# Attention scores in chunks of 256 queries, and one full-array product for values and softmax sums

## The chip, the cores and the metric

The kernel runs on one core of a Trainium2 chip, as one launch. The metric is the device time of that core in microseconds (us). A core has five engines with their own instruction queues, which here do the following: TensorE (PE in the profile, with PEld for its weight loads) multiplies matrices, VectorE (DVE) and ScalarE (ACT) work on the results, GpSimd (POOL) issues the loads that convert types, and SyncE (SP) issues the other transfers. TensorE writes its results to PSUM, which has eight banks; one bank holds 512 fp32 numbers in each of 128 partitions. Each engine takes its instructions strictly in the order in which the program gives them to it.

## The reference

Eight batches of attention with eight heads, 576 positions, 64 numbers per head, and a bias that depends only on the distance between query and key; then a feed-forward layer whose hidden part is the maximum of three products.

```python
scores = (q @ k.transpose(0, 1, 3, 2)) / sqrt(64)          # 8 x 8 x 576 x 576
scores = scores + bias_table[bucket(|i - j|)]              # one number per distance and head
attn = exp(scores - max) ; attn = attn / attn.sum(-1)
x = (attn @ v)  as  4608 tokens x 512
h = maximum(maximum(x @ w1, x @ w2), x @ w3)               # 4608 x 768
out = h @ w_out                                            # 4608 x 512, fp32
```

## The kernel before

The kernel computes scores transposed: keys lie in the partitions and queries along the row, so that the exponentials can be the moving operand of the product with the values. The bias becomes a factor: exp(score) is multiplied by exp(bias), and since the bias is constant beyond a distance of 128, only a band of three 128-wide blocks needs the multiplication (`band`, made at the start from the table by way of `w_sb`, a DRAM buffer `w_dr` and the skewed reload `hank`).

The work goes by 32 pairs of heads: 8 batches times 4 head pairs. The 576 positions of a pair are four key tiles of 128 (`KT`) and a tail of 64 keys; the two heads' tails share the 128 partitions of one "tail" tile. Queries are cut into two halves of `QC` = 288. For one pair the program does this:

- `transpose_q` and `transpose_k` (L325 to L343): ten 128x128 transposes on PE into the PSUM tiles `tq` and `tk`, and two DVE copies to `qT` and `kT`.
- `scores` (L345): the tail tile gives two full-array products of 288 columns (`et`); each of the four key tiles times two query halves gives two products of 288 columns, one per head. Each head contracts over 64 partitions, so the two lie in the upper and lower half of the array's rows ("64\*128" in the profile) and run at the same time. One ACT instruction makes the exponential of 2 x 288 numbers (L363), and DVE multiplies the part within the band (L368, L375).
- `attend` (L386), once per query half: the sum of the exponentials (`den`, with weights of ones) and the product with the values (`o`). Each has one full-array product for the tail, then eight of 64 output columns ("128\*64"), two heads side by side in the array's columns, that run in pairs. ACT makes 1/den as exp(-ln(den)) (L404, L406) and DVE multiplies (L408) into `xT`, the input of the feed-forward.

The feed-forward works on nine chunks of 512 tokens (`ffn_units`, L255): 18 groups of four 512-column products (L90 `ps`), of which every third is copied by ACT (L274) and the others are joined by DVE with a maximum (L277, L280), and four groups of six products for the output, copied by DVE or ACT (L303, L305) and stored by SP. A chunk is cut into 96 single products, which `fill` pours between the pieces of attention by a table of rates; chunk n is poured while batch n + 1 is in attention, and the last two chunks stand at the end. TensorE's instructions are kept in the order in which the program writes them; a scheduler orders the other engines' instructions at build time.

PSUM: `ps_s` has two tiles of two banks for the scores, `ps_a` one bank each for `o` and `den` (used by the transposes too), `ps_f` two banks for the feed-forward.

## Time and profile before

| | us |
|---|---|
| median of 3 runs (415.25 to 417.08) | 415.8 |
| profiled execution, whole | 415.32 |
| its span, first to last instruction | 413.5 |
| PE busy in the span | 379.2 |
| DVE busy | 241.4 |
| ACT busy | 250.7 |
| one batch in the middle (four pairs), period | 44.75 |
| end part: the last two feed-forward chunks | 43.34 |

The profile gives, for a group of instructions, the line, the engine, the operation, output and inputs by the program's names, the shape, the count, the busy time, the mean length of one in ns, and the idle time in front of them with what ended it. A timeline row is a start, a length, and how many instructions are merged in it. Matmuls are pipelined: one of 512 columns is shown 380 ns long although the next starts sooner, so the spacing of starts, not the length, is what a matmul costs in a stream. Most matmuls have the line of a helper, L90, and are told apart by their tiles.

### The profile page before, as it was taken

The page shows a single profiled execution, that of the slowest core. Times are in us where ns is not written, and L with a number is a line of the kernel's source. Part 1 is how long each engine was busy: PE and PEld are TensorE (multiplying, and loading weights), DVE is VectorE, ACT ScalarE, POOL GpSimd, SP SyncE. Part 2 cuts the span into 40 slices and gives each one's busy share as a digit, 9 for nine tenths or more (in the row PEclk, how much of TensorE's full clock was granted, in tenths as well). Part 3 has the DMA queues.
Part 4 walks back from the last instruction along what each step waited for, and adds up shares of the span by engine and source line. Part 5 has one row for each costly group of instructions (what it writes and reads, how often), then busy time and mean ns, then how long its engine had stood idle before and what let it go on. Part 6 is the DMA issues. An engine that isn't in the chain of part 4 may idle for free.

```text
span 413.5 us, 7525 instructions
## 1 busy us (share of the span) xinstructions
PE 379.2 (92%) x2912; PEld 177.9 (43%) x2912; DVE 241.4 (58%) x589; ACT 250.7 (61%) x476; POOL 113.4 (27%) x147
## 2 busy tenths in 40 slices
PE   1488799999999999999999999999999999999995
PEld 1144444444444444444444444444444444444442
DVE  7653556566666665565656666666556565554342
ACT  1565866766766666766676667667676667732221
POOL 8893570804053131604080405312000000000000
PEclk9999999999999999999999999999999999999999
DMA  9999990946469290919094647928001100020202
GB/s 138 191 132 209 168 120 2 90 52 106 30 42 74 103 58 3 113 52 109 0 94 49 106 29 46 70 104 58 0 2 51 52 2 1 27 76 2 102 0 103
DMA packets 121931, 28.61 MB, mean 69 GB/s; under 512 B 113952, under 2 KB 117288, under 8 KB 121896
## 3 DMA queue, kind: packets, MB, share of 16 engines
q0 software_dynamic: 110544, 16.72, 56.3%
q1 hardware_dynamic: 11352, 11.42, 8.3%
q8 instruction: 23, 0.38, 0.4%
q14 instruction: 12, 0.10, 0.1%
HBM read 35.39 MB, written 9.45 MB: 108 GB/s over the span
## 4 chain that ended last, share of the span: by engine, by line
PE 81%; ACT 10%; DMA 2%; issue 2%; DVE 2%; SPq 1%; DVEq 0%
PE ps L90 43%; PE den L90 13%; PE sc L90 11%; PE o L90 9%; ACT e L363 6%; ACT m L274 3%; PE tk L93 2%; PE tq L93 2%; DMA hank<-w_dr 2%; DMA w_dr<-w_sb 1%; SPq L154 1%; ACT rd L406 1%; ACT ld L404 1%; SPq L149 0%; DVE kT L342 0%
## 5 line engine op out<-in xcount | busy, mean ns | idle before, releaser
L363 ACT ACTIVATE e<-sc 128x576 bf16<-128x576 f32 x256 | 152.3, 648 | 100.7 <-PE sc L90 100.5
L90 PE MATMUL ps<-xT,w_bf 128*128 128x512 bf16 x648 | 163.2, 380 | 9.8 <-ACT m L274 9.8
L375 DVE TENSOR_TENSOR e<-e,band 128x576 bf16<-128x576 bf16 (+5 forms) x224 | 80.0, 358 | 90.6 <-ACT e L363 84.7
L90 PEld LDWEIGHTS <-w_bf 128*128 128x128 bf16 x648 | 55.4, 97 | 86.2 <-issue 38.4
L90 PE MATMUL sc<-qT,kT 64*128 64x288 bf16 (+1 forms) x576 | 71.0, 297 | 11.7 <-DVE kT L342 6.1
L90 PEld LDWEIGHTS <-kT 64*128 64x128 bf16 (+1 forms) x576 | 21.9, 95 | 73.3 <-issue 59.5
L90 PE MATMUL ps<-wo_bf,hT 128*128 128x512 bf16 x216 | 52.8, 380 | 0.0
L118 POOL DMA_DIRECT2D q_sb<-in_q_dram x32 | 28.1, 889 | 84.2 <-PE tk L93 76.5
L277 DVE TENSOR_TENSOR m<-ps,m 128x512 bf16<-128x512 f32 x54 | 37.1, 687 | 22.2 <-PE ps L90 16.0
L408 DVE TENSOR_TENSOR xT<-o,rd 128x288 bf16<-128x288 f32 x64 | 29.3, 458 | 35.0 <-ACT rd L406 31.9
L274 ACT ACTIVATE m<-ps 128x512 bf16<-128x512 f32 x54 | 32.5, 602 | 22.2 <-PE ps L90 22.2
L90 PE MATMUL den<-e,ones 128*64 128x288 bf16 x512 | 44.6, 297 | 0.0
L90 PE MATMUL o<-e,v_sb 128*64 128x288 bf16 x512 | 43.1, 291 | 0.0
L280 DVE TENSOR_TENSOR hT<-ps,m 128x512 bf16<-128x512 f32 x54 | 37.1, 688 | 3.5
L122 POOL DMA_DIRECT2D vtail<-in_v_dram x18 | 11.1, 626 | 82.7 <-PE o L90 77.2
L90 PEld LDWEIGHTS <-ones 128*64 128x64 bf16 x512 | 23.9, 110 | 18.4 <-issue 17.0
L404 ACT ACTIVATE ld<-den 128x288 f32<-128x288 f32 x64 | 26.3, 412 | 8.7 <-PE den L90 8.7
L90 PEld LDWEIGHTS <-v_sb 128*64 128x64 bf16 x512 | 29.5, 112 | 2.8
L406 ACT ACTIVATE rd<-ld 128x288 f32<-128x288 f32 x64 | 28.3, 443 | 2.0
L90 PEld LDWEIGHTS <-hT 128*128 128x128 bf16 x216 | 18.5, 97 | 24.3 <-issue 7.0
L118 POOL DMA_DIRECT2D v_sb<-in_v_dram x32 | 28.5, 926 | 0.4 <-issue 0.4
L363 ACT ACTIVATE et<-sc 128x576 bf16<-128x576 f32 x32 | 21.2, 663 | 11.9 <-PE sc L90 11.1
(48 smaller groups left out, 242.3 us busy)
## 6 DMA issues: line engine op xcount, KB each, us to landing
out_dram<-osb SPq DMA_DIRECT2D x36, 256.0 KB, 2.0
q_sb<-in_q_dram POOLq DMA_DIRECT2D x28, 128.0 KB, 4.1
k_sb<-in_k_dram POOLq DMA_DIRECT2D x28, 128.0 KB, 4.0
v_sb<-in_v_dram POOLq DMA_DIRECT2D x28, 128.0 KB, 3.8
w_bf<-in_moe_w_dram POOLq DMA_DIRECT2D x3, 768.0 KB, 11.4
k<-in_k_dram SPq DMA_DIRECT2D x8, 128.0 KB, 3.5
wo_bf<-in_moe_w_out_dram POOLq DMA_DIRECT2D x1, 768.0 KB, 17.4
hank<-w_dr SPq DMA_DIRECT2D x1, 576.0 KB
```

Source lines behind the costliest of these rows:

```text
L90: tc.keep_in_program_order(nc.tensor.matmul(*args, **kw))
L93: tc.keep_in_program_order(nc.tensor.transpose(*args))
L118: nc.gpsimd.dma_start(out=dst[:, t, h0:h1, :], in_=x[:, t, h0:h1, :])
L122: nc.gpsimd.dma_start(out=dst[b % 2][64 * par : 64 * par + 64, h0 // 2 : h1 // 2, 64 * par : 64 * par + 64], in_=src[b, h0 + par : h1 : 2, ...
L274: nc.scalar.activation(out=st["m"][:], in_=ps[:], func=ACTF.Copy)
L277: nc.vector.tensor_tensor(out=m1[:], in0=ps[:], in1=st["m"][:], op=ALU.max)
L280: nc.vector.tensor_tensor(out=hT[:, cf, :], in0=ps[:], in1=st["m"][:], op=ALU.max)
L363: nc.scalar.activation(out=e[:], in_=sc[:, :, 0:QC], func=ACTF.Exp, scale=inv_sqrt_d)
L375: nc.vector.tensor_tensor(out=e[:, :, lo - c * QC : hi - c * QC], in0=e[:, :, lo - c * QC : hi - c * QC], in1=band[hp][:, :, lo - P * t + ...
L404: nc.scalar.activation(out=ld[:], in_=den[:, 0:QC], func=ACTF.Ln)
L406: nc.scalar.activation(out=rd[:], in_=ld[:], func=ACTF.Exp, scale=-1.0)
L408: nc.vector.tensor_tensor(out=xT[hp][:, x0 : x0 + QC], in0=o[:, 0:QC], in1=rd[:], op=ALU.mult)
```

## The change

Scores are computed in two "visits" per pair, each over 256 queries (`QS`), with two key tiles and both heads in one PSUM tile of two banks, so that one exponential takes 2 x 2 x 256 numbers. The 64 queries left over (`left_queries`) and the tail keys (`left_keys`) get products of their own over the full array. All exponentials of a pair go into one tile `e4`, which leaves `attend` free to read query halves of 288 as before.

The values are stored as `vx`: for each head 64 columns of values and 64 columns of ones beside them, so one full-array product gives both the sum over the values and the sum of the exponentials, in the two halves of the partitions of one bank per head (`a0`, `a1`). The tail's product is a pair of row-tiled ones (`attend_open`) put directly behind a visit, which is row-tiled too. The logarithm is now two ACT instructions over 64 partitions (L418), the last multiplication two DVE instructions (L423).

The pair order changes: a pair's two `attend` calls run in the next pair, one behind each visit. The transposes of q and k go to one score tile (`tp`) behind the second visit. The feed-forward is cut into portions of whole groups, of which one goes behind each visit's `attend`; `left_keys` or `left_queries` stands before the last group of the portion. A portion in the middle of a chunk is: third product of a hidden block (`second`), first product of the next (`first`), then, behind the left-over scores, the middle one (`middle`). The end part takes the first two products from the two-bank score tiles. The startup has more set in program order, k is cast partly by ACT, and the constants of the second buffer set are written later.

```diff
-    ep = ctx.enter_context(tc.tile_pool(name="ep", bufs=16))
-    etp = ctx.enter_context(tc.tile_pool(name="etp", bufs=3))
+    ep = ctx.enter_context(tc.tile_pool(name="ep", bufs=3))
...
+    def constants(i):
+        inorder(nc.vector.memset(qtail[i][:], 0.0))
+        inorder(nc.vector.memset(ktail[i][:], 0.0))
+        inorder(nc.vector.memset(vt[i][0:64, :, D:], 1.0))
+        inorder(nc.vector.memset(vt[i][64:128, :, 0:D], 1.0))
+        inorder(nc.vector.memset(vx[i][:].rearrange("p t (h c) -> p (t h) c", c=P)[:, :, D:], 1.0))
...
+    load_hank(0, 2)
+    load_k32(4, H)
+    load_hank(2, H)
...
+        portions = [[f[0], m[0]]] + [[g[cf - 1], f[cf], m[cf]] for cf in range(1, FCH)]
+        portions += [[g[-1], o[0]], o[1:3]]
+        return portions, o[3:]
...
+    def fill(between=None):
+        groups = pending.pop(0) if pending else []
+        for group in groups[:-1]:
+            group()
+        if between:
+            between()
+        for group in groups[-1:]:
+            group()
...
+    def transposes(b, hp):
+        tp = ps_s.tile([P, 2, 2 * CH], BF16, tag="sc", name="tp")
...
+    def visit(qT, kT, e4, c):
+        for tt in range(0, KT, 2):
+            sc = ps_s.tile([P, 2, 2, QS], F32, tag="sc", name="sc")
+            for t in range(2):
+                for par in range(2):
+                    r = slice(64 * par, 64 * par + 64)
+                    mm(
+                        sc[:, par, t, :], lhsT=kT[r, P * (tt + t) : P * (tt + t) + P],
+                        rhs=qT[r, c * QS : c * QS + QS],
+                    )
+            exp(e4[:, tt : tt + 2, :, c * QS : c * QS + QS].rearrange("p t h q -> p h t q"), sc[:])
+
+    def left_keys(qT, kT, et):
+        sc = ps_s.tile([P, 2 * CH], F32, tag="sc", name="sct")
+        kd = kT[:, KT * P :]
+        mm(sc[:, 0:QM], lhsT=kd, rhs=qT[:, 0:QM])
+        mm(sc[:, QM:S], lhsT=kd, rhs=qT[:, QM : QM + 64], start=True, stop=False)
+        mm(sc[:, QM:S], lhsT=kd, rhs=qT[:, QM + 64 : QM + 128], start=False, stop=True)
+        exp(et[:], sc[:, 0:S])
+
+    def left_queries(qT, kT, e4):
+        sc = ps_s.tile([P, KT, 2, 64], F32, tag="sc", name="scq")
+        for t in range(KT):
+            mm(sc[:, t, :, :], lhsT=kT[:, P * t : P * t + P], rhs=qT[:, QM : QM + P])
+        exp(e4[:, :, :, QM:S], sc[:])
+
+    def attend_open(b, hp, c, et):
+        x = [ps_a.tile([P, CH], F32, tag=f"a{par}", name=f"a{par}") for par in range(2)]
+        for par in range(2):
+            r = slice(64 * par, 64 * par + 64)
+            mm(
+                x[par][:, 0:QC], lhsT=vt[b % 2][r, hp, :], rhs=et[r, c * QC : c * QC + QC],
+                start=True, stop=False, skip_group_check=True,
+            )
+        return x
+
+    def attend(b, hp, c, x, e4):
+        for par in range(2):
+            v0 = (2 * hp + par) * P - 64 * par
+            for t in range(KT):
+                mm(
+                    x[par][:, 0:QC], lhsT=vx[b % 2][:, t, v0 : v0 + P],
+                    rhs=e4[:, t, par, c * QC : c * QC + QC], start=False, stop=(t == KT - 1),
+                    skip_group_check=True,
+                )
+        for par in range(2):
+            r, d = slice(64 * par, 64 * par + 64), slice(64 - 64 * par, 128 - 64 * par)
+            nc.scalar.activation(out=ld[r, :], in_=x[par][d, 0:QC], func=ACTF.Ln)
+        nc.scalar.activation(out=rd[:], in_=ld[:], func=ACTF.Exp, scale=-1.0)
...
-    RATES = (6.0, 3.0, 6.5, 4.0, 4.5)
...
+        visit(qT, kT, e4, 0)
+        if before:
+            x = attend_open(*before[0], 0, before[2])
+            attend(*before[0], 0, x, before[1])
...
+        times_band(hp, e4, 0, 0, QS)
...
+        fill(lambda: left_keys(qT, kT, et))
...
+        visit(qT, kT, e4, 1)
+        if before:
+            x = attend_open(*before[0], 1, before[2])
+            attend(*before[0], 1, x, before[1])
+        times_band(hp, e4, 1, 0, 3 * P)
+        times_band(hp, e4, 2, P, 4 * P)
...
+        if ahead:
+            nxt = transposes(*ahead)
...
+        fill(lambda: left_queries(qT, kT, e4))
+        times_band(hp, e4, 3, 2 * P, S)
```

The order of the instructions moves with it, and two places matter. The first is TensorE from the end of a run of scores into the product with the values, for a pair in the middle. In these rows `kT` holds the transposed keys, `ones` and `onesd` are the weights that sum, `vtail`, `vt` and `vx` are values. Before:

```order
L90 MATMUL sc<-qT,kT 128x288
L90 LDWEIGHTS onesd
L90 MATMUL den<-et,onesd 128x288
L90 LDWEIGHTS vtail_97
L90 MATMUL o<-et,vtail_97 128x288
L90 LDWEIGHTS ones
L90 MATMUL den<-e,ones 64x288
```

And now, at the same place, with `a_2074` and `a_2075` for the banks of the two heads:

```order
L94 MATMUL sc<-qT,kT 128x256
L94 LDWEIGHTS vt_96
L94 MATMUL a_2074<-et,vt_96 128x288
L94 LDWEIGHTS vt_96
L94 MATMUL a_2075<-et,vt_96 128x288
L94 LDWEIGHTS vx_94
L94 MATMUL a_2074<-e_1867,vx_94 128x288
```

The array's form goes from row-tiled to full to column-tiled before, and from row-tiled to full now; the tail's products have joined the row-tiled run.

The second place is VectorE from the last band multiplications of a pair to the end of the next feed-forward group. `hT` is the DVE maximum that empties the PSUM bank of a block's third product, `m` the one that empties the middle product's. Before, in the second half of a pair:

```order
L408 TENSOR_TENSOR xT_240<-o,rd 128x288
L280 TENSOR_TENSOR hT<-ps,m_1806 128x512
L375 TENSOR_TENSOR e<-e,band_195 128x2x224
L375 TENSOR_TENSOR e<-e,band_195 128x576
L332 COPY qT<-tq 128x576
L368 TENSOR_TENSOR et<-et,bandt_200 128x192
L342 COPY kT<-tk 128x640
L277 TENSOR_TENSOR m_1910<-ps,m_1867 128x512
L280 TENSOR_TENSOR hT<-ps,m_1910 128x512
```

And now, for a pair with feed-forward in both halves:

```order
L289 TENSOR_TENSOR m<-ps_1493,m_1486 128x512
L355 TENSOR_TENSOR e_1441<-e_1441,band_194 128x2x384 x2
L348 COPY qT<-tp 128x640
L348 COPY kT<-tp 128x640
L423 TENSOR_TENSOR xT_201<-a_1513,rd 64x288
L423 TENSOR_TENSOR xT_201<-a_1514,rd 64x288
L294 TENSOR_TENSOR hT<-ps_1549,m 128x512
L355 TENSOR_TENSOR e_1441<-e_1441,band_194 128x2x320
L289 TENSOR_TENSOR m<-ps_1568,m_1560 128x512
```

In the second half of a pair, the two largest band multiplications, both copies of the transposes and both final multiplications now stand in front of `hT`.

More of the change, by code (lines that the diff above doesn't have):

```diff
@@ L61 @@
     QC = S // 2
+    QS = 2 * P
+    QM = 2 * QS
     KT = 4
@@ L169, in load_tiles @@
         k_sb = loads.tile([P, KT, H, D], BF16, tag="k_sb", name="k_sb")
-        v_sb = loads.tile([P, KT, H, D], BF16, tag="v_sb", name="v_sb")
-        return q_sb, k_sb, v_sb
+        return q_sb, k_sb
     batch = [None] * B
@@ L241 @@
+    ready = {n: (n * CH + CH - 1) // S for n in range(NCH)}
+    pairs = [(b, hp) for b in range(B) for hp in range(HP)]
+    cast_k32(0, 2, act_copy)
+    nxt = transposes(0, 0)
+    cast_k32(2, 4, dve_copy)
+    constants(1)
     batch[1] = load_tiles()
-    load_q(1, 0, H, batch[1])
-    load_k(1, 0, H, batch[1])
+    load_q(1, 0, H)
+    load_k(1, 0, H)
     w_bf = []
@@ L410 @@
-    ready = {n: (n * CH + CH - 1) // S for n in range(NCH)}
-    RATES = (6.0, 3.0, 6.5, 4.0, 4.5)
-    pairs = [(b, hp) for b in range(B) for hp in range(HP)]
-    late = []
-    made, factors = [], []
-    nxt = (transpose_q(0, 0), transpose_k(0, 0))
+    before = None
     for i, (b, hp) in enumerate(pairs):
@@ L456 @@
-    fill(8)
-    while late:
-        late.pop(0)()
+            load_q(b + 2, 0, H)
+            load_k(b + 2, 0, H)
+        fill(lambda: left_queries(qT, kT, e4))
+        times_band(hp, e4, 3, 2 * P, S)
+        before = ((b, hp), e4, et)
+    for c in range(2):
+        x = attend_open(*before[0], c, before[2])
+        attend(*before[0], c, x, before[1])
+        fill()
     for n in range(NCH):
         if ready[n] == B - 1:
-            pending.extend(ffn_units(n))
+            add_ffn(n, True)
```

391 lines of the change are left out of this document (157 added, 234 removed).

## The prediction, made before the changed kernel had run

> **What bounds the kernel now.** I read the page first, then the busy times by stage, TensorE's timeline in the middle, the groups by shape, and the end of the chain that ended last. Of the page, the span, the busy line and the granted clock by slices:
>
> ```profile
> span 413.5 us, 7525 instructions
> PE 379.2 (92%) x2912; PEld 177.9 (43%) x2912; DVE 241.4 (58%) x589; ACT 250.7 (61%) x476; POOL 113.4 (27%) x147
> ...
> PEclk9999999999999999999999999999999999999999
> ```
>
> By stage, with PE, PEld, DVE, ACT and POOL busy in that order, one batch cut at its period:
>
> ```profile
> 189.75:234.50 44.75, 43.35 (x354) 20.38 (x352) 27.60 (x64) 30.26 (x58) 13.71 (x18) 1.00 0.69 64
> ```
>
> A batch takes 44.75 us, a pair 11.19, and PE is busy 43.35 of it: PE bounds. What a matmul costs there is in the spacing of starts. TensorE's timeline in that batch:
>
> ```profile
> 231.61 0.42 PE L90 MATMUL sc<-qT,kT 64*128 64x288 bf16 x4
> 231.96 0.30 PE L90 MATMUL den<-et,onesd 128*128 128x288 bf16 x1
> 232.09 0.29 PE L90 MATMUL o<-et,vtail 128*128 128x288 bf16 x1
> 232.31 0.68 PE L90 MATMUL den<-e,ones 128*64 128x288 bf16 x8
> 232.82 0.66 PE L90 MATMUL o<-e,v_sb 128*64 128x288 bf16 x8
> 233.41 0.82 PE L90 MATMUL ps<-xT,w_bf 128*128 128x512 bf16 x3
> 234.17 0.42 PE L90 MATMUL sc<-qT,kT 64*128 64x288 bf16 x4
> 234.52 1.25 PE L90 MATMUL ps<-xT,w_bf 128*128 128x512 bf16 x5
> 236.24 0.59 PE L90 MATMUL ps<-xT,w_bf 128*128 128x512 bf16 x2 [0.47 <-ACT m L274]
> ...
> 241.00 0.39 PE L93 MATMUL tq<-ident,q_sb 128*128 128x128 bf16 x4
> ...
> 241.56 1.46 PE L90 MATMUL ps<-xT,w_bf 128*128 128x512 bf16 x6
> ```
>
> And the end part, from the chain that ended last:
>
> ```profile
> 366.07 43.34 PE ps L90 x192
> ```
>
> A full-array product of 288 columns takes 0.13 (232.09 - 231.96). Eight `den` take 0.51, so two side by side share one pass of 0.13. One of 512 columns takes 0.216: 43.34 / 192 = 0.226 with that part's waits, and 0.13 x 512 / 288 = 0.23 at most; I take off the waits. Where the array's form changes, about 0.09 is lost: `o` to `den` 0.22 instead of 0.13, `o` to `ps` 0.59 instead of 0.51, two passes of scores 0.35 instead of 0.26, three `ps` before scores 0.76 instead of 0.65. The ten transposes take 0.56. A wait on ACT delays PE by 236.24 - 234.52 - 5 x 0.216 = 0.64. In the list of waits (total, times, longest) it is
>
> ```profile
> PE ps L90 <- ACT m L274: 9.8, 21, 0.5
> ```
>
> 21 times for 28 pairs with feed-forward: three in four.
>
> One pair before: four runs of scores at 0.35 and 0.09 to enter, 1.76; two `attend` at 0.13 + 0.22 + 0.51 + 0.59, 2.90; tail scores 0.25; transposes 0.56; 24 products of feed-forward 5.18; the wait 0.48. Sum 11.13, against 11.19.
>
> **What the change does to PE.** Two visits of four passes, each 0.128 x 256 / 288 = 0.114, are 0.91. The openers, row-tiled, add a pass per visit, 0.26. Sixteen full-array products of 288 columns at 0.125 are 2.00, as many passes as `den` and `o` took beside the tail's. The form changes four times, 0.36, instead of twelve. Left keys (640 columns) 0.28, left queries (512) 0.22, transposes 0.56, feed-forward 5.18. Sum 9.77, where it was 10.65 without the wait.
>
> The Trainium skill, TensorEngine Tiling, section When to Use Tiling, speaks against part of this: weights of 64 columns should be tiled side by side. By that rule alone the value products would double, 1.0 more per pair. But the ones in the other half replace the `den` products, and the rows above count the same passes.
>
> **What is late next.** The other engines' rows, by shape:
>
> ```profile
> L363 ACT ACTIVATE e<-sc 128x576 bf16<-128x576 f32 x256 | 152.3, 648 | 100.7 <-PE sc L90 100.5
> L274 ACT ACTIVATE m<-ps 128x512 bf16<-128x512 f32 x54 | 32.5, 602 | 22.2 <-PE ps L90 22.2
> L375 DVE TENSOR_TENSOR e<-e,band 128x576 bf16<-128x576 bf16 x64 | 29.3, 458 | 5.9 <-ACT e L363 0.5
> L406 ACT ACTIVATE rd<-ld 128x288 f32<-128x288 f32 x64 | 28.3, 443 | 2.0
> L404 ACT ACTIVATE ld<-den 128x288 f32<-128x288 f32 x64 | 26.3, 412 | 8.7 <-PE den L90 8.7
> L342 DVE COPY kT<-tk 128x640 bf16<-128x640 bf16 x32 | 15.4, 483 | 0.0
> L375 DVE TENSOR_TENSOR e<-e,band 128x320 bf16<-128x320 bf16 x32 | 10.4, 325 | 22.1 <-ACT e L363 22.0
> ```
>
> How soon one follows another, from a timeline of all engines:
>
> ```profile
> 192.01 0.42 PE L90 MATMUL sc<-qT,kT 64*128 64x288 bf16 x4
> 192.35 1.19 ACT L363 ACTIVATE e<-sc 128x576 bf16<-128x576 f32 x2 [0.91 <-PE sc L90]
> ...
> 194.36 0.46 DVE L408 TENSOR_TENSOR xT<-o,rd 128x288 bf16<-128x288 f32 x1 [0.52 <-ACT rd L406]
> 194.73 0.68 DVE L280 TENSOR_TENSOR hT<-ps,m 128x512 bf16<-128x512 f32 x1
> ```
>
> ACT starts 0.34 after the pass that it reads starts; its second exponential starts 0.10 before the first ends (2 x 0.648 - 1.19); DVE overlaps by 0.09. The trace has no exponential of 1024 numbers: ACT grows by (648 - 412) / 288 = 0.82 ns each, so 648 + 448 x 0.82 = 1.02. Band multiplications grow by (458 - 325) / 256 = 0.52 ns, so 768 numbers take 0.56. Both go beyond the largest shape seen; a rival below prices that.
>
> I follow a pair with feed-forward in both halves, from its first visit. PE: visit 0.46, opener 0.13, change 0.09, eight products to 1.68; `second` and `first` to 3.41; left keys 3.69; `middle` 4.55; second visit from 4.65; `attend` to 6.33; transposes 6.89; `second` and `first` 8.62; left queries 8.84; `middle` would end at 9.70, the next pair begin at 9.80.
>
> In the first half nothing stops PE. ACT has both exponentials done at 2.4, the logarithms (two now, 0.31 net each) and `rd` at 3.5; DVE's two final multiplications free `a0` and `a1` at 4.3, wanted at 5.1. `middle` takes the bank of `second`, which DVE empties by 3.4, wanted at 3.69. Closest is the ring of two score tiles: the second half of the second visit, at 4.88, needs the tail's exponential out; ACT copies `first` till 4.2, then does the tail till 4.77. It fits by 0.1.
>
> In the second half DVE's order decides. Its band multiplication for key tile 2 waits for the second visit's second exponential, which starts at 4.65 + 0.11 + 0.34 + 0.92 = 6.02 and ends at 7.04. Then DVE does, each less 0.09: the band 0.47, `qT` 0.40, `kT` 0.40, two final multiplications 0.37 each, from 7.07 to 9.08, and only then `hT`, to 9.77. PE's `middle` needs the bank that `hT` empties and stands in PE's queue from 8.84; it starts at 9.82, and all behind it is 0.98 late: 10.78. In a batch's first pair an output copy has `hT`'s place, with the same 10.78. The last pair's second half has ten products and no `middle`: 9.80 - 2 x 0.216 = 9.37. A batch takes 3 x 10.78 + 9.37 = 41.7, against 44.75.
>
> **The two ends.** DVE's first bands that wait for the second `hank`, and TensorE's start, with one `den` run in the first stage and one later, and the first tail scores of the third and fifth pair:
>
> ```profile
> 17.19 0.36 DVE L237 COPY band<-hank 128x768 bf16<-128x768 bf16 x1 [0.55 <-DMA hank<-w_dr]
> ```
> ```profile
> 26.27 1.17 PE L90 MATMUL den<-e,ones 128*64 128x288 bf16 x8
> ...
> 29.49 0.64 PE L90 MATMUL sc<-qT,kT 128*128 128x288 bf16 x2 [0.50 <-ACT e L363]
> ...
> 35.32 0.68 PE L90 MATMUL den<-e,ones 128*64 128x288 bf16 x8
> ...
> 51.02 0.40 PE L90 MATMUL sc<-qT,kT 128*128 128x288 bf16 x2 [0.68 <-ACT e L363]
> ```
>
> The second `hank` now stands behind six k loads on SP's queue and comes some 3 to 4 late, with the other bands behind it on DVE; so I leave the third pair at 29, although the first scores start earlier. Then the old order pays back five owed `attend`; the new one runs 8.5 to 9 a pair without feed-forward: ACT's work is four exponentials at 0.92, 1.0 for tail and left queries, 1.2 for logarithms and 0.9 for `rd`, 6.8, and about 2 go by while DVE makes the last multiplications and the copy that starts the next pair. Batch 1 begins at 47 instead of 51.0 (43 if the late `hank` costs nothing, 51 if it costs twice that). Its first pair has eight products of feed-forward, 8.6: batch 1 takes 39.5, to 86.5; six batches of 41.7 reach 336.8. Then come two `attend` 2.6, 18 products left over 3.9, 192 products 41.5 and a wait of 1.0 for the last pair's bands and banks: 385.8. After the last product 413.5 - 409.4 = 4.1 remain: span 389.9. The profiled execution was 415.32, 1.8 over its span, and 0.5 under the median: **392 us**.
>
> **Rivals.** (1) The stall at `middle` is much smaller, because copies and multiplications on DVE are shorter than these rows: 20 pairs x 0.98 less, 372. Against it: the order is fixed, and the rows are steady. 0.12. (2) The score ring closes: the 0.1 of slack at the tail's exponential is gone, because ACT reaches it 0.6 later; PE waits 0.5 in each of 28 pairs, 14 more, 406. For it: ACT is the engine with least room in that half. 0.20. (3) The exponential with reordered output is slow, and ACT and the chain behind it become the bound: at 1.6 us instead of 1.02 the second exponential ends 1.16 later, three pairs take 11.94, the last 10.2 by ACT's sum (four exponentials 6.0, tail and left queries 1.0, four logarithms 1.2, two `rd` 0.9, a copy and a half 0.9, gaps 0.2): 46.0 a batch, 7 x 4.3 = 30 more and some 4 in batch 0: 426, slower than before. It decides from about 1.45 on. Against it: runs of 256 stay contiguous. 0.08. (4) The clock falls back. The eight `den` at 26.27 take 1.17, those at 35.32 0.68, so PE ran at about half speed at first although the page grants full clock; a later wait of 0.68 (51.02) did not bring that back. If waits of 1 a pair did, with 3.4 us at half speed in each pair, 1.7 x 28 = 48 more: 440. The Trainium skill, TensorE: Matmul & The Clock Gate, Part 1, section on PSUM-queue depth-cycling, says that frequent small idles between groups can make the clock oscillate; no run here shows it. 0.02. (5) Ring and stall together eat the gain, or the start loses it: within 0.5% of 415.8. 0.05.
>
> **How the numbers follow.** The forecast has 0.53, with 382 to 400 from the start's bounds and 0.3 either way per pair. Half a per cent is about what a measurement here can tell. Faster: 0.53 + 0.12 + 0.20 = 0.85; same 0.05; slower 0.10. The range takes in rivals 1 and 2: 370 to 408.
>
> **What would show it.** Right: 41.7 a batch; PE waiting about 1 us for DVE's `hT` once in three pairs of four; four form changes a pair; exponentials of 1.02. Wrong: PE waiting before scores on ACT (2); exponentials of 1.4 or more (3); matmuls at double spacing in the middle (4); batch 1 starting after 51.

## The result, and the profile after

| | before | after |
|---|---|---|
| median of the runs compared, us | 415.58 (7525 instructions) | 402.88 (6692 instructions) |
| ratio, 95% interval | | 0.9685 (0.9652 to 0.9717) |
| profiled execution: whole, span | 415.32, 413.5 | 401.81, 400.0 |
| batch 1 begins in the span | 51.02 | 53.27 |
| one batch in the middle | 44.75 | 42.12 |
| from the end of the last batch, by its period, to the end of the span | 49.23 | 51.53 |

The change makes the kernel 3.15% faster (2.8 to 3.5). The table says where: seven batches give 18.05 us (from 51.02 to 413.5 - 49.23 = 364.27 before, 313.25; from 53.27 to 400.0 - 51.53 = 348.47 after, 295.2), the start takes 2.25 back and the end part 2.30. Sum -13.5, which is 400.0 - 413.5.

The page of the changed kernel, its span, its first busy line and the clock by slices:

```profile
span 400.0 us, 6692 instructions
...
PE 349.6 (87%) x2560; PEld 191.5 (48%) x2560; DVE 264.4 (66%) x554; ACT 272.0 (68%) x447; POOL 118.6 (30%) x156
...
PEclk9999998999999999999999999999999999999999
```

One batch of it, by stage (PE, PEld, DVE, ACT, POOL busy, then the granted clock):

```profile
180.01:222.13 42.12, 39.77 (x309) 22.12 (x310) 30.07 (x61) 32.89 (x54) 14.28 (x18) 1.00 0.73 68
```

PE was busy 43.35 of 44.75; now it is busy 39.77 of 42.12. So its work fell by 3.6 a batch, and 1 of that came back as idle time. What it waits for is in the list of waits (total, times, longest), the lines that concern the steady batches:

```profile
PE ps L94 <- ACT m L280: 6.5, 14, 0.5
PE pso L94 <- DVE hT L294: 5.9, 8, 0.9
...
PE ps L94 <- DVE xT L423: 1.7, 4, 0.5
```

Before, ACT's copy carried the stall of three pairs in four. Now there are three causes, in different pairs. The pairs of a batch take 11.01, 10.36, 10.36 and 10.38. In the second and third, the second half, from a timeline of all engines:

```profile
198.72 1.03 PE L94 MATMUL ps<-xT,w_bf 128*128 128x512 bf16 x4
...
199.58 0.39 PE L94 MATMUL scq<-qT,kT 128*128 128x128 bf16 x4
...
199.78 0.60 ACT L280 ACTIVATE m<-ps 128x512 bf16<-128x512 f32 x1 [0.43 <-PE ps L94]
...
200.36 0.69 DVE L294 TENSOR_TENSOR hT<-ps,m 128x512 bf16<-128x512 f32 x1
200.43 1.02 PE L94 MATMUL ps<-xT,w_bf 128*128 128x512 bf16 x4 [0.46 <-ACT m L280]
```

The row at 198.72 is `first`, the one at 200.43 `middle`. PE is done with the left queries at 199.58 + 0.22 = 199.80 and starts `middle` 0.63 later, just after ACT's copy ends (200.38). DVE's `hT`, which the prediction named, starts at 200.36 and ends at 201.05: `middle` does not wait for it, so it stands in the bank of `first`, not of `second`. The fourth pair, and the next batch's first pair, on PE:

```profile
177.55 1.24 PE L94 MATMUL pso<-wo_bf,hT 128*128 128x512 bf16 x5
179.69 0.39 PE L94 MATMUL pso<-wo_bf,hT 128*128 128x512 bf16 x1 [0.90 <-DVE hT L294]
```
```profile
188.14 0.81 PE L94 MATMUL ps<-xT,w_bf 128*128 128x512 bf16 x3
189.35 0.38 PE L94 MATMUL ps<-xT,w_bf 128*128 128x512 bf16 x1 [0.40 <-DVE xT L423]
189.56 0.38 PE L94 MATMUL scq<-qT,kT 128*128 128x128 bf16 x4
190.07 0.81 PE L94 MATMUL ps<-xT,w_bf 128*128 128x512 bf16 x3
```

The sixth product of the first `output` could start at 177.55 + 5 x 0.216 = 178.63 and starts at 179.69: 1.06 late, for the block of `hT` that the last `second` has just made. In the first pair the fourth product of `first` is 0.56 late, for the `xT` of the pair before, and `middle` 0.28 late.

The sizes that the prediction had worked out from smaller shapes, from the groups by shape:

```profile
L361 ACT ACTIVATE e<-sc 128x1024 bf16<-128x1024 f32 x128 | 124.0, 1021 | 55.5 <-PE sc L94 55.5
...
L355 DVE TENSOR_TENSOR e<-e,band 128x768 bf16<-128x768 bf16 x64 | 35.6, 557 | 17.9 <-ACT e L361 17.8
```

They are the forecast 1.02 and 0.56. The start is where the gain leaks. DVE in the first pair, then PE in the third:

```profile
18.13 0.90 DVE L185 CAST k_sb<-k 128x1024 bf16<-128x1024 f32 x1 [1.50 <-DMA k<-in_k_dram]
20.44 0.27 DVE L185 CAST ktail<-kt 64x128 bf16<-64x128 f32 x1 [1.41 <-DMA kt<-in_k_dram]
21.30 0.23 DVE L185 CAST ktail<-kt 64x128 bf16<-64x128 f32 x1 [0.59 <-DMA kt<-in_k_dram]
...
23.30 0.48 DVE L348 COPY kT<-tp 128x640 bf16<-128x640 bf16 x1
```
```profile
33.73 0.61 PE L94 MATMUL sc<-qT,kT 64*128 64x256 bf16 x8 [1.72 <-DVE kT L348]
...
36.15 0.39 PE L94 MATMUL sc<-qT,kT 64*128 64x256 bf16 x4 [0.33 <-ACT e L361]
37.68 0.39 PE L94 MATMUL sc<-qT,kT 64*128 64x256 bf16 x4 [1.14 <-ACT et L361]
38.50 0.89 PE L94 MATMUL a<-et,vt 64*128 64x288 bf16 x2 [0.42 <-DVE xT L423]
```

The copy to `kT` that starts the second pair stands on DVE behind casts of heads 4 to 7, which wait for their transfers; the second pair begins at 23.84, the third at 33.73, the fourth at 44.15. And the clock falls back twice where there is no feed-forward yet, in the third pair and in the first half of batch 1's first pair (granted clock behind the five engines):

```profile
38.00:42.00 4.00, 3.48 (x22) 2.08 (x20) 2.03 (x4) 2.71 (x5) 0.61 (x1) 0.57 1.16 209
...
58.00:62.00 4.00, 3.74 (x21) 2.49 (x21) 1.66 (x4) 2.59 (x5) 2.41 (x4) 0.60 0.31 20
```

A clock of 0.57 over 4 us is half the clock for (1 - 0.57) x 4 / 0.5 = 3.4 us. The clock record of the trace has the first fall at 38.35 us and the second at 58.83.

### The profile page after: what moved, and what is told of

Same layout as the page of the kernel before. It is cut to its first block, busy times and chain, and to the rows that moved or that the text cites. A ratio compares the mean times of both kernels' runs of the same rounds, so it can differ in the third digit from the quotient of the medians.

```text
span 400.0 us, 6692 instructions
## 1 busy us (share of the span) xinstructions
PE 349.6 (87%) x2560; PEld 191.5 (48%) x2560; DVE 264.4 (66%) x554; ACT 272.0 (68%) x447; POOL 118.6 (30%) x156
## 4 chain that ended last, share of the span: by engine, by line
PE 68%; DVE 13%; ACT 12%; issue 3%; DMA 2%; SPq 1%; DVEq 0%
PE ps L94 32%; PE a L94 15%; ACT e L361 8%; PE pso L94 8%; PE sc L94 8%; DVE xT L423 3%; PE tp L97 3%; ACT m L280 2%; PE sct L94 2%; DVE e L355 2%; DVE qT L348 2%; DVE kT L348 2%; DVE hT L294 1%; DMA kt<-in_k_dram 1%; DVE osb L305 1%
## 5 line engine op out<-in xcount | busy, mean ns | idle before, releaser
L361 ACT ACTIVATE e<-sc 128x1024 bf16<-128x1024 f32 x128 | 124.0, 1021 | 55.5 <-PE sc L94 55.5
L355 DVE TENSOR_TENSOR e<-e,band 128x768 bf16<-128x768 bf16 (+2 forms) x128 | 64.7, 506 | 43.6 <-ACT e L361 43.3
L94 PE MATMUL a<-e,vx 128*128 128x288 bf16 x512 | 76.6, 294 | 0.0
L423 DVE TENSOR_TENSOR xT<-a,rd 64x288 bf16<-64x288 f32 x128 | 58.3, 455 | 22.8 <-ACT rd L419 20.9
L418 ACT ACTIVATE ld<-a 64x288 f32<-64x288 f32 x128 | 51.9, 405 | 10.1 <-PE a L94 6.7
L94 PEld LDWEIGHTS <-vx 128*128 128x128 bf16 x512 | 45.8, 100 | 26.7 <-issue 15.7
L94 PE MATMUL pso<-wo_bf,hT 128*128 128x512 bf16 x216 | 52.7, 379 | 5.9 <-DVE hT L294 5.9
L94 PE MATMUL sc<-qT,kT 64*128 64x256 bf16 x512 | 41.4, 279 | 16.7 <-DVE kT L348 11.9
L289 DVE TENSOR_TENSOR m<-ps,m 128x512 bf16<-128x512 f32 x54 | 37.3, 691 | 17.4 <-ACT m L280 15.1
L134 POOL DMA_DIRECT2D vx<-in_v_dram x32 | 28.2, 917 | 1.0 <-PE a L94 1.0
L134 POOL DMA_DIRECT2D k_sb<-in_k_dram x28 | 25.1, 947 | 1.2 <-DMA q_sb<-in_q_dram 1.2
```

The source lines that it names most:

```text
L94: inorder(nc.tensor.matmul(*args, **kw))
L134: nc.gpsimd.dma_start(out=dst[:, t, h0:h1, :], in_=x[:, t, h0:h1, :])
L289: nc.vector.tensor_tensor(out=st["m"][:], in0=st["ps"][1], in1=st["m0"][:], op=ALU.max)
L355: nc.vector.tensor_tensor(out=e4[:, t, :, lo:hi], in0=e4[:, t, :, lo:hi], in1=band[hp][:, :, lo - P * t + P : hi - P * t + P], op=ALU.mult,)
L361: nc.scalar.activation(out=out_, in_=in_, func=ACTF.Exp, scale=inv_sqrt_d)
L418: nc.scalar.activation(out=ld[r, :], in_=x[par][d, 0:QC], func=ACTF.Ln)
```

## The experiments

Each run's median stands beside the kernel before on the same chip (415.86 to 416.62). Theory A throughout: the steady batches wait at places that the order of the portions and the engines' in-order queues set, and the start waits for transfers, which a cold clock then makes dearer. The rival changes from run to run.

### The swap in the second halves

```diff
-        [[g[cf - 1], f[cf], m[cf]] for cf in range(1, FCH)]
+        [[f[cf], g[cf - 1], m[cf]] if cf in (2, 4) else [g[cf - 1], f[cf], m[cf]] for cf in range(1, FCH)]
```

> Only in the portions of cf 2 and 4 (second halves of the second and third pair of a batch) `first` stands ahead of `second`. Theory A (in these halves `middle` waits 0.63 for ScalarE's copy of `first`, whose bank it was given; with `second` between them the copy is done): the pairs 2 and 3 of a batch go from 10.36 to 9.75, the batch from 42.11 to 40.9, seven batches give 8.7: 394 (393 to 396). Rival (the wait only moves: to `second`, whose bank or operand is then late, or to the next visit): pairs at 10.3 or more, 402 to 404.

Measured: 394.32, ratio 0.9493 (0.9462 to 0.9524); pairs 11.01, 9.81, 9.81, 10.38, batch 41.02. The same place, all engines:

```profile
164.77 0.58 ACT L280 ACTIVATE m<-ps 128x512 bf16<-128x512 f32 x1
...
165.09 0.39 PE L94 MATMUL scq<-qT,kT 128*128 128x128 bf16 x4
165.40 1.02 PE L94 MATMUL ps<-xT,w_bf 128*128 128x512 bf16 x4
...
165.87 0.69 DVE L294 TENSOR_TENSOR hT<-ps,m 128x512 bf16<-128x512 f32 x1
```

The copy ends at 165.35, and `middle` starts 0.09 behind the left queries, well before `hT`. So ACT's copy was the wait, and DVE's `hT` is not on PE's path here: theory A held. A pair without the wait takes 9.81. That is PE's work alone but for under 0.1: `middle` starts 0.31 after the first of the left queries, and in the changed kernel's fourth pair the next product follows them after 0.23 (177.32 and 177.55).

### The swap everywhere

```diff
-        [[g[cf - 1], f[cf], m[cf]] for cf in range(1, FCH)]
+        [[f[cf], g[cf - 1], m[cf]] for cf in range(1, FCH)]
```

> The changed kernel with the two groups ahead of the left-over scores swapped: the next block's first product, then the block's third product, then the middle one. Theory A (what delays the middle product in a pair's second half is ScalarE's copy of the first product, because the allocator gave the middle product that bank): the copy now has a whole group more, so the 0.63 us go in the second and third pair of each batch: 2 x 0.63 x 7 = 8.8 less, 394. Theory B (as the prediction had it, the maximum that empties the third product's bank, late in VectorE's order, is what counts): it starts at about 9.3 us after the pair's first score and ends at 10.0, and the middle product waits for it as before or longer: 402 to 404.

Measured: 407.47, ratio 0.9795 (0.9768 to 0.9822), slower than the changed kernel; batch 42.77. The wait leaves the second halves, and a new one comes in the first:

```profile
208.85 0.44 ACT L419 ACTIVATE rd<-ld 128x288 f32<-128x288 f32 x1
208.97 0.44 PE L94 MATMUL sct<-qT,kT 128*128 128x512 bf16 x3
209.20 0.58 ACT L280 ACTIVATE m<-ps 128x512 bf16<-128x512 f32 x1
...
209.83 1.02 PE L94 MATMUL ps<-xT,w_bf 128*128 128x512 bf16 x4 [0.42 <-ACT m L280]
```

Here ACT comes to the copy late, behind two logarithms and `rd`; PE is ready at 208.97 + 0.28 = 209.25. The second and third pair so exchange one wait for another (10.36 and 10.40), and the fourth, which had none of the first kind, grows from 10.38 to 10.96 by this wait of 0.58. That makes 7 x 0.65 = 4.6; neither theory had it. Batch 1 also began later (54.69), which the swap can hardly have caused (see the run that moves an `output`). The better order of the two products differs between the halves.

### The opener behind the eight products

The two row-tiled products of the tail close the sum instead of opening it, so that the array's form changes four times more per pair; products and operands are the same.

```diff
-                start=True, stop=False, skip_group_check=True,
+                start=False, stop=True, skip_group_check=True,
...
+        attend_close(b, hp, c, et, x)
```

> The changed kernel with the tail's two row-tiled products put behind the eight full-array ones instead of ahead of them, where they continue the visit's form. Same products and sums, four form changes more per pair. Theory (a change of the array's form costs 0.09 us of TensorE, and TensorE's sequence sets the time): 4 x 0.09 x 32 = 11.8 more, 414 to 415, so that nearly all of the gain is gone. Rival (the changes hide behind the waits that TensorE has anyway): under 4 more, 403 to 407.

Measured: 411.21, ratio 0.9882 (0.9846 to 0.9919), batch 43.39:

```profile
185.65:229.04 43.39, 41.47 (x309) 21.48 (x309) 30.35 (x61) 33.38 (x54) 14.32 (x18) 1.00 0.71 66
```

PE's busy time grows by 41.47 - 39.77 = 1.70 for sixteen changes, 0.106 each; the second and third pairs grow by 0.43, 0.108 for each of their four. In the first and fourth, where there are waits, half of it disappears in them (0.21). The prediction's 0.09 was near, and the opener's place directly behind the visit pays: the medians differ by 8.3, and seven steady batches give 7 x 1.27 = 8.9. The total lies between the theory's range and the rival's.

### Values and ones side by side, alone

The kernel before, with `vx`, the row-tiled opener, two logarithms and two last multiplications; scores, order and portions are as before.

```diff
-        for dst in (den, o):
...
-                        lhsT=ones[:] if dst is den else v_sb[:, t, 2 * hp + par, :],
+                    x[par][:, 0:QC], lhsT=vx[b % 2][:, t, v0 : v0 + P],
```

> The kernel before with the second half of the change alone: values and ones side by side, full-array products, row-tiled openers behind the scores, two logarithms and two last multiplications; score chunks of 288, the schedule and the pouring of the feed-forward stay as before. Theory (the gain is TensorE's form changes and passes in the value part): per half 1.80 us of scores and attend become 1.48, 0.64 per pair, 20 in all less what the longer logarithms and multiplications give back at TensorE's waits: 396 to 401, as fast as the whole change or faster. Rival (the value part pays only with the new schedule, because ScalarE and VectorE get 0.6 and 0.7 us more per pair): 408 to 416.

Measured: 413.76, ratio 0.9947 (0.9927 to 0.9967). The start and one batch of it:

```profile
35.00:69.00 34.00, 27.09 (x126) 12.68 (x126) 13.20 (x34) 18.31 (x38) 10.81 (x14) 0.50 1.13 105
98.13:141.21 43.08, 40.68 (x290) 20.02 (x288) 30.99 (x73) 33.59 (x68) 13.68 (x17) 1.00 0.71 66
```

The batch is 43.08 (42.6 later), 1.7 to 2.2 below that of before, and most of what the whole change reaches. But in the start the clock is at half for 34 us and batch 1 begins only at 63.63 (51.02 before), so the whole kernel gains only half a per cent. The total alone would have said that this part is worth nothing. What the steady batches of the whole change have beyond it, some 0.5 to 1.0, belongs to the score chunks and the new order together; no run parts these two.

### The same, with dummy products in the first batch

```diff
+        if not pending and warm[0] is not None:
+            wps = ps_f.tile([P, CH], F32, tag="ff", name="wps")
+            for _ in range(int(mms / 2)):
+                mm(wps[:], lhsT=warm[0][:, 0:P], rhs=warm[0][:, 0:CH])
```

> The kernel before with values and ones side by side, as tried alone, and dummy products of 512 columns (as many as half the portion, none in steady batches) where its first batch has no feed-forward. Theory (values and ones alone were worth 1.36 per batch, and half the clock over 34 us of the start took most of it back): the clock stays full, the whole 403 to 408. Rival (the loss lies in ScalarE's and VectorE's waits of the start, the dummies add to it): 412 to 418.

Measured: 408.92, ratio 0.9828 (0.9799 to 0.9856).

```profile
35.00:69.00 34.00, 28.15 (x185) 13.39 (x186) 16.61 (x43) 24.39 (x50) 14.34 (x18) 0.90 1.40 123
```

The clock is at 0.90 in the same stretch, the steady batches are the same 43.09, and the time falls by 4.8 although TensorE has more to do. The expected range missed by 1. Batch 1 begins at 57.71, where it was 63.63 without the dummies and 51.02 in the kernel before: about half of the start's loss went with the dummies, and 6.7 us stay. In part these are waits for VectorE, as the rival had it: TensorE waits twice for 1.45 until `xT` is out of the bank that the next opener takes (at 36.85 and 40.85).

### Dummy products in the changed kernel

Six products at each of the nine places where the changed kernel has no portion (the first four pairs and half of the fifth).

```diff
+        if not groups and warm[0] is not None:
+            wps = ps_f.tile([P, CH], F32, tag="ff", name="wps")
+            for _ in range(6):
+                mm(wps[:], lhsT=warm[0][:, 0:P], rhs=warm[0][:, 0:CH])
```

> Six dummy products of 512 columns into a bank of the feed-forward ring, never read, at each place of the first four pairs and a half where there is no feed-forward portion (about 1.3 us of TensorE each, ten places); they change nothing else. Theory A (the granted clock falls to half in the first batch because TensorE idles between products there, and costs 2 to 3 us): the clock stays full from about 28 on, batch 1 begins at 51 to 52 instead of 53.3, the whole 400 to 402. Rival (the waits of the first batch are set by VectorE and ScalarE; the clock matters little, the dummies stand in the way): batch 1 at 53 to 56, the whole 403 to 406.

Measured: 399.84, ratio 0.9618 (0.9587 to 0.9649).

```profile
38.00:42.00 4.00, 3.37 (x34) 2.19 (x34) 2.54 (x6) 3.91 (x7) 0.61 (x1) 1.00 1.15 208
...
58.00:62.00 4.00, 2.84 (x26) 1.95 (x26) 3.01 (x6) 2.50 (x6) 3.78 (x5) 1.00 0.66 42
```

With the full clock the third pair takes 8.95 instead of 10.42, and the first of batch 1 9.81 instead of 11.41. The fourth, which had the full clock before too, takes 8.94 instead of 9.13. The run with the swap in the second halves has the third pair at full clock and without dummies: 9.13. So of the third pair's 1.47 the clock is 1.29. Early on the dummies cost 1.3 (third pair at 35.05 instead of 33.73), so batch 1 begins at 52.94, only 0.3 earlier and later than theory A had it; the rest of the gain comes in its first pair. Adding work made the kernel 3 us faster.

### Casts one pair later, and the second `hank` ahead of k

```diff
-        if i == 0:
+        if i == 1:
             cast_k32(4, H, dve_copy)
```

> The changed kernel with one line moved: VectorE casts the k of the last four heads one pair later, so the copies that start the second pair no longer stand behind them. Theory (the start eats part of the gain, because VectorE's in-order casts wait for the late k transfers): in the changed kernel the second pair's scores start at 23.84 us, after casts that wait till 21.3; with the casts gone from there, bands, two large band multiplications and the two copies follow from 17.2 on, so the second pair starts at 19 to 20 and the whole is 3.5 to 4.5 us shorter: 398.5 to 399.5. Rival (the late second hank transfer holds the second pair instead): it starts earlier, but the third pair stays at about 33.7, and the time stays within 1 us of 402.9.

Measured: 401.73, ratio 0.9662 (0.9638 to 0.9687). The second pair begins at 18.83 instead of 23.84, the third at 34.07 instead of 33.73. The five microseconds are lost again, above all on DVE, whose next band waits for the second `hank`, as the rival had it (the clock is also at half, from 26.8 to 37.0):

```profile
23.08 0.63 DVE L248 COPY band<-hank 128x768 bf16<-128x768 bf16 x2 [3.91 <-DMA hank<-w_dr]
```

The interval of the ratio overlaps that of the changed kernel (0.9652 to 0.9717), so no gain is shown. The next run has the later casts and, on SP's queue, the second `hank` ahead of the six loads of k:

```diff
-    load_k32(4, H)
     load_hank(2, H)
+    load_k32(4, H)
```

> The first six band columns (the second `hank` transfer) are sent ahead of the loads of k heads 4 to 7, and the casts of those heads stand one pair later on VectorE. Theory A (the start of the changed kernel is late because VectorE's in-order queue holds first the casts that wait for k, then, with the casts moved, the band products that wait for `hank`): with both gone the second pair begins near 19 as in the run with the casts moved alone, the third near 28 instead of 34, batch 1 at 48 to 49 instead of 52.7 to 53.3, the whole 398 (396 to 400). Rival (what is late is the data of the next pairs, q and k by GpSimd's queue, or the clock): the third pair stays at 33 or later and the time at 401 to 403.

Measured: 399.25, ratio 0.9609 (0.9579 to 0.9639). The time lies where theory A had it, the mechanism does not: the third pair begins at 32.66, not near 28, and the second at 22.77, not near 19. What holds the second pair now is on DVE:

```profile
18.94 0.66 DVE L248 COPY band<-hank 128x768 bf16<-128x768 bf16 x1 [2.14 <-DMA hank<-w_dr]
...
21.84 0.48 DVE L348 COPY qT<-tp 128x640 bf16<-128x640 bf16 x1
22.24 0.48 DVE L348 COPY kT<-tp 128x640 bf16<-128x640 bf16 x1
```

The copy of the second pair's band from the second `hank` now stands on DVE ahead of the first pair's band multiplications. It waits until 18.94, and from there DVE is busy without a gap until `kT` is copied. With the casts moved alone, that copy stood behind the start of the second pair. The tail of q comes late too (its transpose starts at 19.27 where it was 16.14), but it is transposed before DVE gets to `qT`; and in the three later runs that send `hank` first it starts at 17.4 to 18.2, where the seven variants of the changed kernel that send it last have 16.1 to 17.9, so the order does not show as its cause. One wait in front of DVE's queue was exchanged for another. Nor is the gain shown to come from here: the profiled execution has batch 1 at 52.23 instead of 53.27, which is less than the start differs by itself (next section).

### Moving products to cover the waits of the fourth and the first pair

The first of three runs moves the first `output` behind the fill with the last `second`, in the changed kernel:

```diff
-        portions += [[g[-1], o[0]], o[1:3]]
-        return portions, o[3:]
+        portions += [[g[-1]], o[0:2]]
+        return portions, o[2:]
```

> The first `output` of a chunk is moved out of the portion that holds the last `second` into the next pair's, the third into the portion after. Theory A (its sixth product waits 1.06 for `hT`, which VectorE makes behind qT, kT and two xT): the fourth pair of a batch loses the wait and the 1.5 of the moved product (10.38 to about 7.8 to 8.0), the first pair takes 1.5 more (11.01 to 12.5), the batch 42.1 to 41.1, the whole 395 to 396. Rival (it is a wait for VectorE that whatever stands next takes over, since the pair is bound by VectorE's and ScalarE's chain of the tail): the batch stays at 42, the whole at 402 to 404.

Measured: 406.05, ratio 0.9771 (0.9724 to 0.9818), slower than the changed kernel and above both expectations. The fourth pair loses 1.52, of which the moved `output` itself is 1.30 (6 x 0.216), and the first takes 1.65 more. PE behind the fourth pair:

```profile
181.34 0.61 PE L94 MATMUL sc<-qT,kT 64*128 64x256 bf16 x8 [0.57 <-ACT e L361]
...
182.95 0.77 PE L94 MATMUL a<-e,vx 128*128 128x288 bf16 x5 [0.37 <-DVE e L355]
```

The wait for `hT` is gone, and the next visit waits for an exponential and then its `attend` for the band instead: with 1.3 less of products between, the score ring closes. A steady batch comes to 42.24, only 0.12 more than in the changed kernel. The profiled execution, the slowest of this run's four, is 6.7 longer than that of the changed kernel: six such batches make 0.7 of this, batch 1 and the end part together 3.5 (one `output` moves from the one to the other, and the clock fell once more, at 351.1), and 2.4 are lost ahead of batch 1.

That last part can hardly be the edit's. Up to batch 1 this run, the two with swaps and the changed kernel give PE, DVE and ACT the same instructions in the same order, and yet batch 1 begins at 55.71, 53.33 (swap in the second halves), 54.69 (swap everywhere) and 53.27. Between the first record of the full clock, at 27 to 28 us, and batch 1 the clock was at half for 10.2, 3.4, 11.0 and 3.4 us in them. So a start can differ by 2.4 us from one profiled execution to the next, and a smaller difference between two starts need not come from an edit.

The second has the improved start and swap (the last run below, which its expectation calls the run before), and the last `second` in the first half:

```diff
+        portions[-1].append(g[-1])
+        portions += [[o[0]], o[1:3]]
```

> As the run before, and the last `second` of a chunk moved into the first half of the fourth pair, so that `hT` is made a half pair ahead of the `output` that reads it; the work of the pair is unchanged. Theory A (the 0.9 to 1.06 that the sixth product of the first `output` waits is the price of VectorE's queue alone): the fourth pair goes from 10.38 to 9.4 to 9.8, the batch to 40.1 to 40.4, the whole 4 to 6 below the run before. Rival (the second half, now shorter by 1.0, closes the score ring as it did when the `output` was moved: 0.57 for the exponential and 0.37 for the band): the fourth pair stays at 10.2 to 10.6, the whole within 1 of the run before.

Measured: 392.23, ratio 0.9421 (0.9391 to 0.9452), 3.2 slower than without the move. The fourth pair falls to 9.80 as theory A said, the first rises from 11.01 to 11.70, so the batch is 41.13 where theory A had 40.1 to 40.4, and the end part has a new wait; neither expectation had the time:

```profile
131.72 0.77 PE L94 MATMUL a<-e,vx 128*128 128x288 bf16 x5 [0.49 <-DVE e L360]
...
336.17 0.28 PE L94 MATMUL a<-et,vt 64*128 64x288 bf16 x1 [1.45 <-DVE xT L428]
```

The third moves the third `output` into the second half of the first pair:

```diff
-        portions += [[g[-1], o[0]], o[1:3]]
-        return portions, o[3:]
+        portions += [[g[-1], o[0]], o[1:2]]
+        return portions, o[2:]
```

> As the start and the swap together, and the third `output` of a chunk moved from the first half of a batch's first pair into its second half, ahead of `first`, whose fourth product waits 0.56 for the xT of the pair before and after which `middle` waits 0.28 for a copy to `osb`. Theory A (these waits are what VectorE's queue costs at this place, and 1.5 of products ahead of them cover it): the first pair of a batch goes from 11.01 to 10.2 to 10.5, the batch from 41.02 to 40.2 to 40.5, the whole 384 to 386. Rival (as in the runs that moved an `output` or a `second`: the first half, now shorter by 1.5, closes the score ring by about 0.9, and the wait only moves): the first pair stays at 10.9 to 11.6, the whole 388 to 393.

Measured: 394.19, ratio 0.948 (0.945 to 0.951), 5.2 above the version without it. The wait for `xT` in the second half is gone, and behind the shortened first half the second visit waits for the exponential and its opener for the bank of `a`:

```profile
135.29 0.39 PE L94 MATMUL sc<-qT,kT 64*128 64x256 bf16 x4 [0.24 <-ACT et L365]
136.10 0.28 PE L94 MATMUL a<-et,vt 64*128 64x288 bf16 x1 [0.42 <-DVE xT L427]
```

The first pair is then 11.77 instead of 11.01. Three different moves give the same answer: right behind the half that gave products away PE waits for ACT or DVE. In the changed kernel the products of that half cover their chain.

### The start and the swap together

The dummy products, the later casts, `hank` ahead of k and the swap in the second halves, as the diffs above show them.

> The dummy products of the first batch, the later casts with the second `hank` transfer first, and the swap in the second halves, together. Theory (the start and the steady part are separate places, each with its own waits): the steady batch is 41.02 as with the swap alone, batch 1 begins at 50 to 52, the whole 388 to 391. Rival (the gains of the start overlap, since each of them takes the same idle time of TensorE): batch 1 at 52 to 53, the whole 391 to 394.

Measured: 389.02 (388.18 to 389.99), ratio 0.934 (0.9308 to 0.9372), the fastest kernel here.

```profile
131.54:172.56 41.02, 39.39 (x305) 22.12 (x309) 29.88 (x61) 32.89 (x54) 14.28 (x18) 1.00 0.76 70
```

Batch 1 begins at 50.70, about where that of the kernel before begins, and the steady batch is that of the swap alone: the two places are separate, as the theory had it.

## Why the prediction was right, and where it failed

Forecast 392, measured 402.88 (profiled 401.81). The direction was right, and so was the main reason, less work on the engine that bounds. But the time is outside the band of the forecast proper, 382 to 400; it lies in the stated 370 to 408 only because that took in rival 2, the closed score ring, which did not happen. That much of it is luck. One of the prediction's own signs of being wrong came too: batch 1 started after 51.

**PE's work: right.** Forecast 9.77 of work and 9.80 for a pair that waits for nothing; with the wait removed it measured 9.81, under 0.1 of it still a wait. The term for the change of form was 0.09, measured 0.106 to 0.108. The Trainium skill, TensorEngine Tiling (Array Packing), section Key Properties, says that a change of tiling mode drains TensorE; it gives no price, and the run with the opener moved is one.

**One size was missed.** A batch holds 96 products of the feed-forward. I followed pairs of 24 and gave the last pair its 22, but the first pair has 26 (two `output` in one half, an `output`, `first` and `middle` in the other). Two products are 0.43. The forecast batch was 41.7, the measured one 42.12: this is the difference.

**The stall: right in sum, wrong in place.** The step that failed is "`middle` takes the bank of `second`". In the second halves it takes that of `first`, and waits for ACT's copy. DVE's order was as forecast (`hT` at 9.08 of the pair; 200.36 - 191.03 = 9.33), but nobody on PE waited for it there. I forecast three stalls of 0.98, 2.94 a batch. By difference to the work the trace has 0.55 in each of two pairs (10.36 - 9.81), 0.77 in the first (11.01 - 9.81 - 0.43) and 1.0 in the last (10.38 - 9.81 + 0.43), 2.9. That the sums agree is chance: they are three causes, of which I had named one, and for the last pair I had none.

**The start: the range for batch 1 did not hold.** Forecast 47 (43 to 51), measured 53.27. The step "I leave the third pair at 29" fell: DVE's casts came before the second pair, and with these out of the way the band did, as the run with the casts moved shows. The step "8.5 to 9 a pair" was near for a full clock (9.13 without dummies) and wrong where the clock fell (10.42). The first pair of batch 1, forecast 8.6, took 11.41; dummies and the clock that they kept up took 1.6 off (9.81), and 3.4 us at half the clock can cost 1.7 at most. Against the forecast span of 389.9 the start and batch 1 lost 6.3 + 3.0, six batches 2.4, and the end part gave 1.6 back: 400.0.

**The rivals.** The score ring (2) did not close in the steady batches of the changed kernel, but it was near, as forecast: two runs closed it by taking products away (waits of 0.57 and 0.24 before scores). The falling clock (4) came, but only where the feed-forward is missing, and for 3.4 us twice, not in every pair. The prediction drew on the Trainium skill, TensorE: Matmul & The Clock Gate, section on PSUM-queue depth-cycling, for frequent small idles, and said that no run showed it; this case's trace now agrees for the start: between 32 and 38.5 PE waited 1.72, 0.33, 1.14 and 0.42, and the clock fell at 38.35, in the last of these waits. Waits of the same lengths between 42.4 and 48.9 were not followed by a fall. Another section of that page of the Trainium skill, Why this matters for your kernels, asks that gaps of more than about 3 us be avoided; from 28.1, where the record first has the full clock, to the second fall at 58.83 none was over 1.72, so by that rule alone the clock would have stayed full, and the trace differs.

**What stays open.** When the clock falls is not settled. The traces show it change in steps of 3.41 us (in the changed kernel it is full for 10.24 from 28.1 on, half for 3.41, full for 17.07, half for 3.41). In the changed kernel's start, cut at these steps, the falls came after stretches in which PE was busy 1.67 and 1.36 of 3.41, and none came after 1.70, 1.69 and 1.85; so it may count how much of a stretch the waits fill, and not how long any one of them is (PE's busy time includes modelled ends, and these figures lie close together). But in the run with values and ones alone a fall came after 2.13, so this is no rule. In that run the next nine stretches were busy 2.10 to 3.14 at half the clock, and it came back only behind one that was busy throughout; in the changed kernel it came back behind 3.17 and 3.41. The kernel before has the full clock on record from 34.8 on (its slow `den` at 26.27 shows half the clock earlier, although the page draws 9 there), and from then to batch 1 its least busy stretch had 2.34. Why the allocator gave `middle` the bank of `first` the runs don't show. The end part's 2.30 was not taken apart.

## What to carry to other kernels

When the bound engine's work shrinks, list for each portion of its stream which bank or operand it takes and which engine frees that; which bank an allocator gives is read from the program, not assumed. Count instructions over a whole period, not over a typical pair. An engine that has just been relieved can be too idle where nothing fills it: look at the granted clock in the start by itself, and judge a part by its steady stage and its start apart, since one can hide the other. Before a start is called better, look how far it differs between runs in which nothing in it was changed; here it was 2.4 us.

## What the runs showed of the hardware

A change between row-tiled and full-array products cost 0.106 to 0.108 us. The granted clock fell to half for 3.4 us at a time after several idle gaps of 0.3 to 1.7 us, without any long one, and in one kernel stayed there for 34 us; with six dummy products of 512 columns at each of the nine places without feed-forward it stayed full from 28.7 on in the changed kernel. In four kernels with the same instructions up to there, batch 1 began at 53.27 and 53.33 where the clock had been at half for 3.4 us, and at 54.69 and 55.71 where it had been for 10.2 to 11.0. An exponential from two banks of 2 x 2 x 256 numbers with its output in another order took 1.021 us, what 0.82 ns per number beyond 576 gives: the reordering costs nothing that can be seen.
